# Sums of v on GpSimd for all pairs, joined bits from the second pair on, and another instruction order for hashed attention with a channel mix behind it

## The chip, the cores and the metric

The kernel runs on one core of one Trainium2 chip. Times are device microseconds (us) of one execution. TensorE is called PE, VectorE DVE, ScalarE ACT and GpSimd POOL, as in the profile. A time "timed" is of an ordinary execution, a "profiled" one of the execution that the trace shows; "span" is the stretch from its first to its last instruction. Every execution also has a mean granted clock of TensorE (1.0 is full speed) and a state, fast or slow (here: over 1.5% above the fastest of the same kernel).

## The reference, cut to what matters

```python
# attention: 4 batches x 8 heads, 768 positions, 64 wide
q_bits = (q @ proj > 0); k_bits = (k @ proj > 0)          # 6 bits each
mask   = bucket(q_bits)[:, None] == bucket(k_bits)[None]   # attend only within a bucket
attn   = softmax(where(mask, q @ k.T / 8, -1e9))
x      = (attn @ v)  laid out as [batch, 768, 512]
# channel mix ("feed-forward" below)
x_prev = x shifted by one position
xk = mu_k * x + (1 - mu_k) * x_prev ;  xr = mu_r * x + (1 - mu_r) * x_prev
k  = relu(xk @ w_k) ;  v = (k * k) @ w_v ;  r = sigmoid(xr @ w_r)
out = r * v                                                # float32
```

## The kernel before

Work comes in 16 pairs of heads, four pairs to a batch; pair 3 ends batch 0, and only when the mix of pair 3 is there can the first feed-forward matmul run. Each pair needs: loads of q, k and v; two DVE operations that split q and k into a float16 high and low part; a DMA transpose (for pairs 0 and 1 a transpose on PE); the hash bits, found by small matmuls and written as extra rows of the operands; nine score blocks and nine exponentials; the weighted sums of v; a division; a transposition; a difference and a mix.

All instructions are first collected as operations with an engine, a priority and an estimated duration. A plan then simulates the engines and emits the instructions in the order that it found. The priorities are a long list of numbers found by search.

```python
WANT = [4, 17, 6, 12, ...]            # 1306 priorities, cut
...
    def schedule(self):
        ...
                if o.tr:               # a DMA transpose
                    dur = max(dur, dma_free - 1.0 - t, tr_free + 0.1 - t)
```

The sums of v over the 768 positions give the mean, which is subtracted from v (pairs 4 to 15) or added as a tiny term (pairs 0 to 3, "uc"):

```python
        def f1(): nc.gpsimd.tensor_tensor(... 128x390 ...)     # three adds, pairs 0 to 3
        def f2(): nc.gpsimd.tensor_tensor(... 128x130 ...)
        def f3(): nc.gpsimd.tensor_tensor(... 128x130 ...)
        def f123():                                            # one reduction, pairs 4 to 15
            nc.vector.tensor_reduce(out=vs, in_=vn.rearrange("p j c d -> p j d c"), axis=X, op=ALU.add)
        ...                       # then: mean on PE, subtraction ("va") and "mc" on DVE
```

Bits are written in one of two ways. `DIRECT` pairs get them on the spot, one DVE operation of 6 rows for each of the four operands. All others get "joined" bits: one DVE operation for all four, `bx`, followed by four small row DMAs that put the rows in place.

```python
    DIRECT = (0, 1)
```

The weights w_r and w_v are staged in float32 in the buffer that later holds the squares of the feed-forward, and cast from there:

```python
    k2_f = k2_all.bitcast(FP32)                      # k2: squares of relu
    ...
        if z < NST: stage = k2_f[:, z * 2 * DM : (z + 1) * 2 * DM]     # w_r 0,2 and w_v 0,2
        else:       stage = wst[...]                                     # w_v 4,6
        add("SP", 0.5, T, f_w, ...)       # the load, named wl4 to wl9
        add("POOL", 1.1, ..., f_c, ...)   # the cast, named wc4 to wc9
```

The softmax here doesn't subtract the row's maximum and nothing guards it: scores larger than these inputs give would overflow.

Of the kernel before, what the change touches and what calls it, by code (L numbers as in the profile page):

```python
# [39 lines left out]
def R(kind, n):  # L40
# [4 lines left out]
    4, 17, 6, 12, 16, 19, 26, 30, 33, 21, 5, 14, 18, 20, 8, 10, 24, 13, 7, 9, 22, 25, 29, 27,  # L45
    23, 70, 31, 32, 34, 37, 38, 28, 74, 2, 41, 122, 57, 65, 127, 252, 271, 299, 321, 353, 378, 287, 307, 390,
    413, 435, 430, 0, 11, 1, 15, 58, 35, 3, 66, 36, 39, 44, 48, 55, 63, 42, 45, 49, 60, 40, 43, 47,
    54, 62, 68, 46, 50, 59, 53, 56, 61, 71, 84, 94, 80, 67, 69, 83, 89, 99, 79, 96, 86, 136, 85, 92,
    98, 102, 77, 72, 78, 100, 123, 141, 51, 52, 64, 88, 106, 111, 76, 93, 101, 73, 126, 133, 87, 117, 129, 139,
    143, 156, 103, 107, 81, 91, 90, 97, 75, 82, 121, 124, 138, 140, 132, 134, 113, 119, 110, 114, 149, 135, 146, 130,  # L50
    151, 145, 152, 155, 170, 177, 182, 197, 209, 212, 224, 221, 109, 128, 105, 104, 108, 112, 115, 95, 125, 142, 118, 144,
    153, 174, 180, 203, 189, 198, 194, 148, 158, 159, 164, 147, 150, 169, 178, 165, 171, 195, 200, 188, 191, 179, 183, 161,
    168, 184, 190, 192, 211, 215, 204, 207, 210, 232, 239, 241, 246, 249, 250, 262, 257, 116, 202, 120, 154, 157, 163, 167,
    131, 137, 162, 160, 166, 175, 199, 205, 245, 225, 234, 217, 226, 231, 235, 237, 248, 253, 229, 259, 238, 242, 213, 219,
    220, 218, 216, 227, 206, 208, 270, 273, 277, 292, 293, 251, 254, 258, 276, 279, 322, 329, 334, 337, 351, 342, 176, 186,
    222, 173, 181, 187, 214, 172, 185, 233, 230, 236, 244, 263, 272, 289, 278, 290, 283, 268, 286, 280, 285, 275, 267, 260,
    269, 256, 264, 288, 312, 282, 291, 298, 301, 243, 247, 294, 302, 309, 314, 324, 313, 317, 326, 332, 347, 352, 359, 363,
    366, 371, 422, 381, 387, 404, 410, 419, 445, 436, 441, 456, 392, 398, 406, 420, 439, 446, 492, 499, 506, 449, 468, 481,
    407, 415, 429, 448, 466, 480, 451, 516, 526, 479, 486, 500, 438, 457, 473, 509, 515, 532, 514, 528, 536, 489, 504, 519,
    476, 483, 494, 524, 531, 533, 548, 571, 578, 505, 510, 574, 587, 605, 612, 577, 581, 561, 563, 588, 623, 636, 650, 632,  # L60
    642, 652, 704, 627, 631, 590, 597, 645, 694, 647, 656, 660, 670, 686, 793, 223, 261, 274, 296, 303, 305, 311, 323, 193,
    196, 201, 228, 240, 265, 295, 300, 330, 297, 343, 320, 316, 325, 344, 348, 335, 333, 339, 341, 328, 349, 304, 308, 310,
    318, 355, 357, 350, 354, 356, 360, 365, 376, 383, 368, 373, 380, 386, 388, 327, 416, 444, 453, 469, 503, 461, 475, 346,
    370, 377, 340, 345, 379, 391, 402, 255, 266, 338, 281, 284, 306, 385, 393, 412, 408, 424, 400, 389, 394, 362, 367, 375,
    382, 403, 409, 395, 401, 372, 374, 414, 426, 397, 421, 417, 433, 423, 425, 427, 434, 458, 465, 467, 474, 478, 484, 442,
    488, 517, 523, 544, 543, 535, 551, 384, 361, 428, 315, 331, 358, 336, 364, 399, 437, 455, 405, 411, 443, 497, 508, 518,
    530, 513, 525, 459, 472, 440, 452, 470, 477, 454, 460, 485, 495, 502, 507, 511, 521, 431, 447, 482, 490, 522, 529, 520,
    539, 547, 537, 540, 546, 553, 558, 369, 562, 583, 595, 601, 609, 611, 658, 319, 396, 463, 418, 491, 557, 564, 568, 450,
    487, 501, 432, 527, 534, 567, 576, 580, 594, 584, 602, 538, 542, 545, 549, 555, 559, 573, 586, 582, 591, 596, 604, 570,
    575, 593, 598, 552, 556, 603, 606, 608, 615, 621, 613, 616, 619, 624, 626, 655, 629, 653, 662, 675, 679, 692, 697, 710,  # L70
    682, 729, 701, 711, 731, 716, 728, 770, 707, 695, 717, 734, 747, 761, 746, 762, 796, 696, 786, 795, 771, 779, 822, 756,
    783, 799, 817, 823, 831, 791, 797, 818, 805, 828, 839, 829, 838, 847, 850, 859, 869, 812, 830, 837, 836, 842, 855, 803,
    810, 870, 874, 883, 887, 785, 794, 888, 895, 903, 913, 833, 890, 867, 886, 917, 925, 926, 933, 919, 912, 936, 945, 967,
    976, 975, 983, 986, 991, 943, 953, 923, 931, 962, 968, 471, 464, 572, 462, 554, 566, 599, 651, 498, 560, 565, 493, 579,
    589, 622, 633, 644, 659, 639, 663, 665, 671, 610, 614, 620, 625, 646, 661, 640, 649, 657, 666, 638, 643, 630, 634, 674,
    684, 678, 680, 683, 688, 693, 723, 725, 727, 733, 735, 767, 742, 773, 777, 784, 790, 787, 792, 496, 541, 617, 512, 654,
    677, 669, 685, 550, 628, 635, 569, 637, 648, 691, 700, 718, 709, 721, 713, 708, 714, 706, 722, 699, 702, 668, 676, 687,
    690, 720, 732, 749, 757, 738, 741, 730, 737, 740, 743, 750, 758, 763, 766, 769, 801, 814, 820, 775, 835, 864, 872, 881,
    889, 876, 897, 600, 607, 698, 592, 705, 712, 724, 754, 585, 641, 673, 618, 703, 726, 778, 800, 815, 808, 811, 821, 760,
    764, 755, 772, 804, 819, 802, 813, 782, 789, 781, 806, 745, 752, 845, 851, 827, 834, 843, 852, 858, 875, 878, 880, 893,  # L80
    899, 907, 910, 774, 915, 929, 932, 940, 944, 935, 977, 689, 667, 788, 664, 826, 856, 848, 862, 672, 719, 751, 715, 739,
    759, 816, 832, 853, 844, 860, 849, 861, 868, 892, 896, 906, 911, 854, 863, 894, 901, 840, 846, 879, 884, 904, 908, 877,
    882, 957, 960, 963, 971, 974, 934, 948, 952, 959, 966, 873, 978, 990, 992, 995, 1001, 999, 1006, 1126, 1130, 1133, 1020, 1025,
    1030, 1078, 1087, 1094, 1042, 1049, 1059, 1132, 1141, 1146, 1026, 1035, 1044, 1095, 1103, 1109, 1047, 1063, 1066, 1122, 1150, 1152, 1110, 1116,
    1121, 1015, 1114, 1119, 1074, 1080, 1084, 1145, 1155, 1157, 1104, 1124, 1128, 1134, 1139, 1143, 1092, 1100, 1111, 1031, 1039, 1162, 1169, 1173,
    1175, 1089, 1091, 1149, 1179, 1176, 1180, 1174, 1182, 1154, 1159, 1185, 1187, 1202, 1207, 1197, 1200, 1209, 1210, 1194, 1198, 1183, 1206, 1215,
    1216, 1212, 1213, 1226, 1229, 1232, 1235, 681, 768, 866, 744, 898, 909, 914, 924, 748, 753, 776, 765, 809, 825, 918, 902, 942,
    954, 937, 949, 981, 985, 916, 920, 964, 970, 980, 982, 955, 961, 972, 979, 930, 941, 950, 969, 939, 946, 994, 998, 1000,
    1004, 1009, 988, 1003, 1005, 1011, 1013, 927, 1017, 1033, 1036, 1055, 1061, 1046, 1054, 736, 798, 922, 841, 938, 947, 956, 965, 780,
    824, 871, 807, 900, 905, 1010, 1016, 1040, 1029, 1023, 1034, 993, 996, 997, 1007, 984, 989, 1045, 1051, 1014, 1018, 1008, 1012, 1038,  # L90
    1043, 1022, 1027, 987, 1002, 1057, 1062, 1069, 1073, 1075, 1050, 1056, 1067, 1072, 1077, 973, 1081, 1097, 1098, 1102, 1115, 1105, 1113, 921,
    1019, 1024, 1021, 1028, 857, 865, 958, 885, 891, 928, 1086, 1090, 1107, 1101, 1112, 1096, 1068, 1076, 1060, 1064, 1106, 1118, 1082, 1085,
    1079, 1083, 1065, 1071, 1053, 1070, 1088, 1093, 1099, 1108, 1137, 1140, 1142, 1147, 1151, 1123, 1117, 1120, 1125, 1127, 1032, 1153, 1165, 1161,
    1166, 1170, 1167, 1214, 951, 1037, 1048, 1041, 1052, 1138, 1144, 1164, 1168, 1148, 1156, 1129, 1131, 1135, 1136, 1181, 1184, 1158, 1160, 1163,
    1171, 1172, 1178, 1177, 1186, 1188, 1190, 1192, 1189, 1191, 1193, 1195, 1196, 1058, 1199, 1201, 1203, 1204, 1205, 1208, 1219, 1224, 1211, 1218,
    1221, 1217, 1222, 1225, 1223, 1227, 1230, 1239, 1244, 1246, 1234, 1238, 1240, 1220, 1228, 1231, 1237, 1241, 1243, 1251, 1256, 1258, 1248, 1253,
    1255, 1245, 1250, 1252, 1242, 1247, 1249, 1257, 1262, 1264, 1260, 1265, 1267, 1254, 1259, 1261, 1266, 1271, 1273, 1263, 1268, 1270, 1274, 1277,
    1272, 1276, 1278, 1280, 1233, 1236, 1269, 1275, 1281, 1284, 1286, 1282, 1287, 1295, 1294, 1296, 1279, 1285, 1283, 1288, 1290, 1291, 1300, 1298,
    1297, 1301, 1304, 1305, 1289, 1292, 1293, 1299, 1302, 1303,
]  # L100


class Op:
    pass


class Plan:
# [15 lines left out]
    def add(self, eng, dur, prio, fn, r=(), w=(), take=None, give=(), lag=None, name="", at=0.0, svc=0.0, off=None, tr=0, port=0):  # L123
        o = Op()
# [789 lines left out]
```

## Time and profile before

| what | before |
|---|---|
| timed, two runs | 261.88 and 261.82 us |
| profiled run: time, span, granted clock | 258.05, 256.3, 0.989 |
| first feed-forward matmul | 69.1 us |
| PE busy ahead of it | 56.4 of 69.1 us |
| PE busy after it, up to PE's end | 180.0 of 182.6 us |
| PE's end to the end of the span | 4.6 us |

The table's last rows come from the busy times by stretch. The columns are: the stretch and its length, then busy us (and instructions) of PE, PE's weight loads, DVE, ACT and POOL, then the granted clock, the DMA share and GB/s. The kernel before:

```profile
0.00:69.10 69.10, 56.44 (x678) 35.33 (x679) 58.75 (x106) 50.08 (x57) 20.72 (x50) 0.98 0.99 242
69.10:251.67 182.57, 180.03 (x1761) 106.50 (x1776) 140.50 (x326) 133.78 (x186) 4.72 (x3) 1.00 0.59 143
251.67:256.30 4.63, 0.00 (x0) 0.00 (x0) 0.69 (x1) 0.00 (x0) 0.00 (x0) 0.77 0.29 113
```

PE stands idle for 12.7 us in the first stretch and for 2.5 us in the second.

One more view of the kernel before, the same columns at 2 us: PE has a bubble at 32 to 36 us, and its clock is granted at half at 36 to 38 us.

```profile
32.00:34.00 2.00, 1.30 (x23) 0.68 (x20) 0.10 (x1) 1.83 (x2) 0.00 (x0) 1.00 1.25 216
34.00:36.00 2.00, 0.78 (x14) 0.43 (x13) 1.79 (x3) 0.04 (x1) 0.00 (x0) 0.92 1.00 294
36.00:38.00 2.00, 2.00 (x20) 1.25 (x17) 1.68 (x5) 0.00 (x0) 0.42 (x1) 0.50 0.83 237
```

### The profile page before, as it was taken

The page shows a single profiled execution, that of the slowest core. Times are in us where ns is not written, and L with a number is a line of the kernel's source. Part 1 is how long each engine was busy: PE and PEld are TensorE (multiplying, and loading weights), DVE is VectorE, ACT ScalarE, POOL GpSimd, SP SyncE. Part 2 cuts the span into 40 slices and gives each one's busy share as a digit, 9 for nine tenths or more (in the row PEclk, how much of TensorE's full clock was granted, in tenths as well). Part 3 has the DMA queues.
Part 4 walks back from the last instruction along what each step waited for, and adds up shares of the span by engine and source line. Part 5 has one row for each costly group of instructions (what it writes and reads, how often), then busy time and mean ns, then how long its engine had stood idle before and what let it go on. Part 6 is the DMA issues. An engine that isn't in the chain of part 4 may idle for free.

```text
span 256.3 us, 6102 instructions
## 1 busy us (share of the span) xinstructions
PE 236.5 (92%) x2434; PEld 141.8 (55%) x2453; DVE 199.9 (78%) x431; ACT 183.9 (72%) x241; POOL 25.4 (10%) x53
## 2 busy tenths in 40 slices
PE   7688978897999999999999989999999999999992
PEld 3445544564665565556575455466575656555440
DVE  3999968799999999998987997995976644755322
ACT  4673939899889966669797976579899866257210
POOL 6181800111023000000000000000000000000000
PEclk9999979999999999999999999999999999999998
DMA  6999999989999978896999966868101013030122
GB/s 180 259 380 230 197 239 208 252 246 209 296 289 228 248 185 175 225 229 139 280 253 178 272 89 166 166 185 171 36 6 33 7 31 120 6 122 3 71 92 82
DMA packets 73291, 43.44 MB, mean 170 GB/s; under 512 B 55520, under 2 KB 68144, under 8 KB 73264
## 3 DMA queue, kind: packets, MB, share of 16 engines
q1 hardware_dynamic: 72608, 42.02, 66.9%
q0 software_dynamic: 576, 1.05, 2.2%
q8 instruction: 19, 0.31, 0.5%
q14 instruction: 8, 0.07, 0.1%
q10 hardware_dynamic: 80, 0.00, 0.0%
HBM read 24.12 MB, written 6.29 MB: 119 GB/s over the span
## 4 chain that ended last, share of the span: by engine, by line
PE 69%; DMA 12%; DVE 9%; SPq 4%; ACT 3%; issue 2%; DVEq 0%; ACTq 0%
PE ps_all L698 16%; PE ps_all L847 16%; PE ps_all L818 13%; PE ps_all L728 11%; PE ps_all L837 7%; DMA a<-bx 5%; PE ps_all L582 4%; DMA a<-nh 3%; ACT pt L702 3%; DMA xt<-ob 2%; DMA nat<-in_k_dram 2%; SPq L595 1%; DVE a L666 1%; DVE vs L517 1%; DVE nh L621 1%
## 5 line engine op out<-in xcount | busy, mean ns | idle before, releaser
L702 ACT ACTIVATE pt<-ps_all 128x1024 bf16<-128x1024 f32 x144 | 141.4, 1031 | 32.5 <-PE ps_all L698 31.5
L698 PE MATMUL ps_all<-a 128*128 128x512 f16 (+1 forms) x384 | 82.3, 327 | 5.2 <-ACT pt L702 2.7
L728 PEld LDWEIGHTS <-pt 128*128 128x128 bf16 x1152 | 44.7, 98 | 8.7 <-issue 0.5
L698 PEld LDWEIGHTS <-a 128*128 128x128 f16 x384 | 32.9, 97 | 28.8 <-issue 9.1
L818 PE MATMUL ps_all<-xk,wk 128*128 128x384 bf16 x256 | 48.0, 326 | 0.4 <-ACT kr L822 0.4
L728 PE MATMUL ps_all<-va,pt 128*128 128x65 bf16 x1152 | 46.7, 194 | 0.1
L847 PE MATMUL ps_all<-wv,k 128*128 128x512 bf16 x181 | 45.8, 379 | 0.6
L822 ACT ACTIVATE kr<-ps_all 128x384 bf16<-128x384 f32 x64 | 30.4, 498 | 7.6 <-PE ps_all L818 5.9
L818 PEld LDWEIGHTS <-wk 128*128 128x128 bf16 x256 | 24.4, 98 | 16.9 <-issue 1.0
L854 DVE SCALAR_TENSOR_TENSOR os<-rs,ps_all 128x512 f32<-128x512 f32 x24 | 16.3, 684 | 19.0 <-PE ps_all L847 12.6
L840 ACT ACTIVATE rs<-ps_all 128x512 f32<-128x512 f32 x24 | 14.4, 599 | 22.8 <-PE ps_all L837 22.7
L847 PEld LDWEIGHTS <-k 128*128 128x128 bf16 x192 | 18.5, 98 | 19.7 <-issue 0.3
L825 DVE TENSOR_TENSOR k<-kr 128x384 bf16<-128x384 bf16 x64 | 21.8, 351 | 9.5 <-ACT kr L822 9.4
L559 DVE SCALAR_TENSOR_TENSOR nh<-nat,nh 128x768 f16<-128x768 f32 x28 | 27.4, 980 | 0.1
L837 PE MATMUL ps_all<-wr,xr 128*128 128x512 bf16 x88 | 24.1, 379 | 0.4
L556 DVE TENSOR_SCALAR nh<-nat 128x768 f16<-128x768 f32 x28 | 15.7, 563 | 4.0 <-DMA nat<-in_q_dram 1.9
L517 DVE TENSOR_REDUCE vs<-vn 128x128 bf16<-128x768 f32 x12 | 17.8, 1479 | 0.3 <-DMA vn<-in_v_dram 0.3
L744 DVE TENSOR_TENSOR ob<-ps_all,rc 128x384 bf16<-128x384 f32 x32 | 17.6, 553 | 0.4
L585 DVE TENSOR_SCALAR bx<-ps_all 128x768 uint16<-128x768 uint16 x14 | 13.3, 953 | 3.3 <-PE ps_all L582 3.1
L837 PEld LDWEIGHTS <-xr 128*128 128x128 bf16 x96 | 9.2, 98 | 10.0 <-issue 0.3
L582 PE MATMUL ps_all<-a,p 128*32 128x256 f16 (+1 forms) x224 | 12.4, 331 | 2.2 <-DMA a<-nh 1.9
L538 DVE SCALAR_TENSOR_TENSOR va<-ps_all,vn 128x384 bf16<-128x384 f32 x24 | 12.8, 545 | 0.2 <-PE ps_all L533 0.2
(67 smaller groups left out, 151.2 us busy)
## 6 DMA issues: line engine op xcount, KB each, us to landing
vn<-in_v_dram SPq DMA_DIRECT2D x16, 384.0 KB
out_dram<-os SPq DMA_DIRECT2D x24, 256.0 KB
nat<-in_k_dram SPq DMA_DIRECT2D x15, 384.0 KB
nat<-in_q_dram SPq DMA_DIRECT2D x15, 384.0 KB
wk<-in_moe_w_k_dram POOLq DMA_DIRECT2D x4, 256.0 KB, 7.8
k<-in_moe_w_r_dram SPq DMA_DIRECT2D x2, 512.0 KB
k<-in_moe_w_v_dram SPq DMA_DIRECT2D x2, 512.0 KB
wst<-in_moe_w_v_dram SPq DMA_DIRECT2D x2, 512.0 KB
```

The source lines that it names most:

```text
L517: nc.vector.tensor_reduce(out=vs, in_=vn.rearrange("p j c d -> p j d c"), axis=mybir.AxisListType.X, op=ALU.add)
L559: nc.vector.scalar_tensor_tensor(out=nh[:, :, D:P], in0=nat.rearrange("p j (c d) -> p (j c) d", d=D), scalar=QS, in1=nh[:, :, 0:D], op0=AL ...
L582: nc.tensor.matmul(ps[32 * i : 32 * i + 32, lo:hi], w_, a_t[sa][:, i, lo:hi], start=st, stop=not st)
L698: nc.tensor.matmul(ps[:, lo - s * STEP : hi - s * STEP], side_a["k"][sa][:, j, jc * P : (jc + 1) * P], side_a["q"][sa][:, j, q0 : q0 + hi ...
L702: nc.scalar.activation(out=pt_t[sp][:, s * STEP : (s + 1) * STEP], in_=ps_t[plan.slot[nm]], func=AF.Exp, bias=EBIAS, scale=ESC)
L728: nc.tensor.matmul(oo[:, ic * 65 : ic * 65 + 65], pt_t[sp][:, o : o + P], va_t[sa][:, j, jc, 0 : D + 1], start=(not uc and ic == 0 and jc ...
L744: nc.vector.tensor_tensor(out=ob_t[so][:, :, j * D : (j + 1) * D], in0=oo[:, :, 0:D], in1=rc_t[sr][:, 1, :].unsqueeze(2).to_broadcast([P, ...
L818: nc.tensor.matmul(ps[:, 0:HALF], wk_sb[:, d, fc * P : (fc + 1) * P], xk_t[mx[d]][:, h * HALF : (h + 1) * HALF], start=(d == 0), stop=(d = ...
L822: nc.scalar.activation(out=kr_t[sk], in_=sm(nm)[:, 0:HALF], func=AF.Relu, scale=0.5 ** 0.5)
L825: nc.vector.tensor_tensor(out=k2_t[s2][:, h * HALF : (h + 1) * HALF], in0=kr_t[sk], in1=kr_t[sk], op=ALU.mult)
L837: nc.tensor.matmul(sm(nr), xr_t[mx[d]][:, c * P : (c + 1) * P], wr_sb[:, d, :], start=(d == 0), stop=(d == NDC - 1))
L847: nc.tensor.matmul(sm(nv), k2_t[(b * NFC + fc) % NK2][:, c * P : (c + 1) * P], wv_sb[:, fc, :], start=(fc == 0), stop=(fc == NFC - 1))
```

## The change

Its intent: take the twelve reductions off DVE, which is the fullest engine early on, and give them to GpSimd, which is idle nine tenths of the time; take the bits of pair 1 from four DVE operations to one; and tell the plan that a DMA transpose behind a backlog of transfers takes longer, then search the order anew.

```diff
-WANT = [4, 17, 6, 12, ...]          # 1306 priorities
+WANT = [6, 17, 10, 0, ...]          # 1328 priorities, all others
...
                 if o.tr:
+                    dma_free += 0.5 * (dma_free > t)
...
+                heapq.heappush(events, (t + dur, 3, o.i))
...
-    DIRECT = (0, 1)
+    DIRECT = (0,)
...
-        add("SP", ..., svc=1.08, name=f"ldq{n}{side}")
+        add("SP", ..., svc=1.13, name=f"ldq{n}{side}")     # and small changes of other estimated costs
...
-        def f123(): ... nc.vector.tensor_reduce(...)
-        if not uc:
-            add("DVE", DVE_C(768), pr, f123, ...)
-        else:
-            add("POOL", 0.85, pr, f1, ...)   # and f2, f3
+        add("POOL", 0.85, pr, f1, ...)       # and f2, f3, for all pairs
```

## The prediction

> **What bounds the kernel now.** I read the busy table first, then stretches of time, then the DVE groups, then the chain of waits and the timelines of the first 70 us.
>
> ```profile
> PE 236.5 (92%) x2434; PEld 141.8 (55%) x2453; DVE 199.9 (78%) x431; ACT 183.9 (72%) x241; POOL 25.4 (10%) x53
> ...
> PE   7688978897999999999999989999999999999992
> ...
> DVE  3999968799999999998987997995976644755322
> ```
>
> TensorE is busy 92% of 256.3 us, and the digits show that nearly all of what is missing lies in the first ten or eleven slices (6.4 us each), before the first feed-forward work. There DVE stands at 9. The stretches make this exact; 69.20 us is where the first feed-forward matmul starts (from the timeline of PE), 251.70 us where PE ends. Columns: stretch, its length, then PE, PEld, DVE, ACT, POOL busy us with counts, granted clock, DMA share, GB/s.
>
> ```profile
> 24.00:32.00 8.00, 7.42 (x106) 4.98 (x106) 7.33 (x11) 6.69 (x8) 5.94 (x7) 1.00 1.05 171
> 32.00:40.00 8.00, 6.08 (x82) 4.06 (x79) 5.57 (x10) 2.96 (x4) 0.42 (x1) 0.79 1.03 228
> 40.00:48.00 8.00, 5.80 (x54) 3.28 (x52) 5.49 (x12) 8.00 (x9) 0.00 (x0) 1.00 1.03 200
> 48.00:56.00 8.00, 7.90 (x129) 5.10 (x127) 7.90 (x13) 7.18 (x9) 1.61 (x1) 1.00 0.97 285
> 56.00:64.00 8.00, 6.43 (x86) 4.24 (x82) 8.00 (x15) 7.47 (x8) 2.08 (x2) 1.00 1.00 211
> ...
> 69.20:251.70 182.50, 179.93 (x1758) 106.45 (x1774) 140.40 (x325) 133.68 (x185) 4.72 (x3) 1.00 0.59 143
> ```
>
> From 69.2 us on PE is full (179.93 of 182.50), whatever the others do: that part can only move as a block. Before it PE is busy 56.5 of 69.2 us, 12.7 us idle. So the kernel's end is "when does feed-forward work start" plus a fixed amount of PE work. Two things set that start. First, at 32 to 40 us ACT has 2.96 us of work: a gap of 4.29 us before its 19th exponential, which waits for the scores of pair 2, and PE waited for the transpose DMA:
>
> ```profile
> 30.01 5.17 DMA a<-nh
> 35.22 1.06 PE ps_all L582 x8
> ```
>
> Second, by the timeline of ACT the 36th exponential (the last of pair 3) ends near 56.8 us, yet the first feed-forward matmul starts 12.4 us later, because its input, the mix of pair 3, is the last of a long DVE queue; 56 to 64 us has DVE at 8.00 of 8.00, with the sums of v in it:
>
> ```profile
> 57.78 1.38 DVE vs L517
> ...
> 60.88 0.54 DVE va L538
> 61.42 0.47 DVE df L785
> 61.88 1.37 DVE vs L517
> 63.26 0.93 DVE xr L791
> ```
>
> **What the Trainium skill says.** "VectorE: DVE Perf Modes", the perf-mode tier table: a tensor_reduce has only the 1x rate. The trace is even worse than one element a cycle: 768 float32 take 1479 ns, while the two-input operation on as many elements takes 980.
>
> ```profile
> L559 DVE SCALAR_TENSOR_TENSOR nh<-nat,nh 128x768 f16<-128x768 f32 x28 | 27.4, 980 | 0.1
> L517 DVE TENSOR_REDUCE vs<-vn 128x128 bf16<-128x768 f32 x12 | 17.8, 1479 | 0.3 <-DMA vn<-in_v_dram 0.3
> L666 DVE TENSOR_SCALAR a<-ps_all 6x768 uint16<-6x768 uint16 x6 | 5.6, 953 | 0.3
> L507 POOL TENSOR_TENSOR vt<-va 128x390 f32<-128x390 bf16 x4 | 3.6, 898 | 0.3
> L510 POOL TENSOR_TENSOR vt<-vt 128x130 f32<-128x130 f32 x4 | 2.0, 499 | 0.3
> ```
>
> "GPSIMD Engine Reference", 3.1, puts a GpSimd add at about twice the Vector engine's time; here 390 columns take 0.85 us undisturbed, and the engine is 90% idle, so twice is cheap. "SBUF — State Buffer", Who interferes with whom: GpSimd shares a port pair with DVE operations that have two SBUF inputs or run in a two-port mode, as an exclusive lock, and tensor_reduce never takes part. The trace agrees: the last add of a pair takes 0.42 us alone and 1.01 us at 27.6 us beside DVE work, and the DVE subtraction of 384 columns takes 1.05 us at 12.3 us beside GpSimd against 0.55 usually. "TensorE: Matmul & The Clock Gate", Part 1: the clock follows recent activity. The trace shows 0.79 in 32 to 40 us, the stretch with the transpose wait, so a bubble there costs more than itself.
>
> **The change part by part.** (1) Twelve reductions leave DVE: 12 x 1479 ns = 17.8 us. Twelve groups of three adds come to GpSimd: 0.85 + 0.42 + 0.42 = 1.7 us, 20 us in all on an engine with 25.4 us of work. Some of it comes back to DVE as lock time; the four groups of the kernel before lengthened DVE operations by some 0.3 us a group (my estimate from the durations above), so 12 x 0.3 = 3.6 us, mostly after 69 us where it does not matter. (2) Pair 1 no longer writes its bits in place: four DVE operations of 0.95 us and 32 small matmuls go; one joined operation (0.9 us), 16 joined matmuls (0.8 us) and four small row DMAs come, which must queue behind other transfers. (3) The plan's cost for a transpose behind a backlog rises, so the whole order is another one. This is the largest part, and it can be read from the built instruction order: the first feed-forward matmul comes after 42 score blocks instead of 48 and before the weighted sums of pair 4; on DVE, everything of v's means (pairs 4 to 6) now stands behind the mix of pair 3.
>
> DVE work that must precede the mix of pair 3: before, from 3.13 to 68.39 us less 6.4 us of waits in the DVE timeline, 58.9 us. Taken away: 4 x 0.95 = 3.8 for the bits, 3 x 1.4 = 4.2 for the sums of pairs 4 to 6 (1.37 to 1.43 start to start), 2.2 for subtracting the means of pairs 4 and 6, moved behind; added 0.9. 58.9 - 9.3 = 49.6 us, so DVE alone would allow 52.7 us.
>
> But the exponentials must also come. I walked the new order by hand with the durations of the trace. The first exponential starts about 0.5 us later (10.9), as DVE does more of pair 1 first. The second head of pair 0 gets its bits near 19 us (29 DVE operations, 14.7 us of work from 3.1 us and 1.5 us of waits) instead of 16.4 to 17.3; so ACT pauses after four exponentials, and the ninth ends near 24.7 us (23.2 before). The rows of pair 1, issued from 17.3 us, should be there by then, and the eighteenth ends near 33.3 us (34.0 before). The bits of pair 2 come near 29.8 us, their rows near 35, so the nineteenth starts near 36 us instead of 38.3, the twentieth near 37 instead of 39.9. At 0.945 us each (11 in 10.40 us) the 36th ends near 53 us. Then the last weighted sum (1.5 us), division, joined bits and second division (2.6), the transposing matmuls behind three score blocks, the copy, the difference and the mix (2.7): the first feed-forward matmul near 60.1 us, 9.1 us earlier than now.
>
> Of that, PE work that now stands behind instead of ahead is paid back: 6 score blocks x 0.43 + the weighted sums of pair 4, 2 x 1.15, + two means, 0.2: 5.1 us. Gain 9.1 - 5.1 = 4.0 us. The tail (PE's end to the span's end, 4.6 us) keeps its length. 261.85 - 4.0 = 257.8 us.
>
> **The rivals.** (a) A DMA wait takes the place of the DVE wait. For it: the DMA share is near 1.0 from 8 to 140 us, total bytes do not fall, four row DMAs are added, and all four weight loads on the GpSimd queue now stand at the start. Then the rows of pairs 1 and 2 come 2 to 4 us later than I took and the gain is 0 to 2 us: 260 to 262. Against it: fewer loads stand ahead of the first transposes in the new order. (b) The plan is now right about transposes and the gap before the nineteenth exponential vanishes altogether: the 36th ends near 51 us, feed-forward starts at 57 to 58, the gain is 6 to 7 us: 255 to 256. For it: the DVE floor of 52.7 us allows it. Against: the bits still take a DVE queue, a small DMA and about 5 us. (c) Later starvation: PE is ahead by several us but pairs 8 to 13 still come at the DMA's pace, and PE idles at 120 to 160 us, where the chain already shows transposes of 3.68 and 4.43 us. That would return 1 to 3 us. (d) GpSimd's in-order queue: sums behind a weight cast that waits for its DMA (the old kernel waited up to 12.7 us there) delay a mean. Unlikely to bind, as v has three buffers and means stand far ahead.
>
> **Range and chances.** 257.8 us, with 254.6 to 260.6 holding it 8 times in 10: (b) sets the low end, (a) and (c) the high one. Faster by 2% means under 256.6, a gain over 5.2 us; with an uncertainty of some 2.7 us around 4.0 that is about one chance in three. Slower by 2% would need a new stall of 9 us in a freshly laid order: 3%.
>
> **What would show it.** Right: the reduction gone, DVE near 180 us busy, POOL near 46; the first feed-forward matmul near 60 us, the gap before the nineteenth exponential under 3 us, the clock at 32 to 40 us above 0.79, PE full after. Wrong if that matmul starts after 63 us, if PE after it is idle by over 4 us more than the 2.6 us now, or if adds on GpSimd average far over 0.6 us and stretch DVE's subtractions above 1.1 us.

## The result, and the profile after

The changed kernel took 258.10 and 257.71 us, 257.9 in the middle, and agrees with the reference. Against the kernel before in the same rounds its ratio is 0.9849, with a 95% interval of 0.9807 to 0.9892. Here and below a ratio is the mean time of one kernel's fast runs over that of the other's fast runs of the same rounds, so it is not quite the ratio of the medians that are quoted. By the mark of 2% that the prediction used, this counts as the same time: the gain is clear of noise, but it is not shown to reach 2%.

The page of the changed kernel: busy times, then PE, DVE and granted clock in 40 slices, in tenths.

```profile
PE 234.8 (92%) x2433; PEld 140.3 (55%) x2453; DVE 186.6 (73%) x416; ACT 182.9 (71%) x241; POOL 48.3 (19%) x89
...
PE   8769987797997999899899999999999999999993
...
DVE  3997889889667986998999848668764656673422
...
PEclk9999999999999999999999999999999999999999
```

DVE lost 13.3 us of work and POOL gained 22.9. A slice is 6.4 us. PE's line now has holes behind the tenth slice: a 7 in the 13th (77 to 83 us), an 8 in the 17th and the 20th, where the kernel before had nines up to the 23rd. The clock line has no dip; that of the kernel before had a 7 in its sixth slice (and an 8 in its last). By stretches, the changed kernel:

```profile
0.00:59.70 59.70, 48.84 (x587) 29.62 (x588) 48.97 (x88) 42.18 (x49) 20.35 (x52) 1.00 0.98 225
59.70:252.42 192.72, 185.92 (x1850) 110.64 (x1867) 136.96 (x328) 140.73 (x193) 27.90 (x38) 1.00 0.65 153
252.42:256.20 3.78, 0.00 (x1) 0.00 (x0) 0.69 (x1) 0.00 (x0) 0.00 (x0) 0.92 0.36 139
```

The four terms: the start came 9.4 us earlier (69.1 to 59.7), PE work after it grew by 5.9 (180.03 to 185.92), idle time of PE after it grew by 4.3 (2.54 to 6.80), the tail shrank by 0.85. The sum is -0.1 us: **the two profiled runs are equally long** (256.3 and 256.2), while the timed runs differ by 4 us. So this pair of profiles cannot explain the gain. One of them, that of the kernel before, is of a run that was far better than its usual.

Why it starts earlier is seen in ACT's timeline (start, length, line, operation, how many; in brackets the idle time before, and what ended it). In the kernel before, the 19th exponential and the eight from the 31st to the 38th:

```profile
38.33 1.02 ACT L702 ACTIVATE pt<-ps_all 128x1024 bf16<-128x1024 f32 x1 [4.29 <-PE ps_all L698]
...
51.01 7.66 ACT L702 ACTIVATE pt<-ps_all 128x1024 bf16<-128x1024 f32 x8 [0.67 <-PE ps_all L698]
```

The changed kernel:

```profile
10.56 3.77 ACT L700 ACTIVATE pt<-ps_all 128x1024 bf16<-128x1024 f32 x4
19.41 13.01 ACT L700 ACTIVATE pt<-ps_all 128x1024 bf16<-128x1024 f32 x14 [5.07 <-PE ps_all L696]
34.27 1.02 ACT L700 ACTIVATE pt<-ps_all 128x1024 bf16<-128x1024 f32 x1 [1.86 <-PE ps_all L696]
36.01 12.02 ACT L700 ACTIVATE pt<-ps_all 128x1024 bf16<-128x1024 f32 x13 [0.71 <-PE ps_all L696]
...
50.36 2.85 ACT L700 ACTIVATE pt<-ps_all 128x1024 bf16<-128x1024 f32 x3 [0.66 <-PE ps_all L696]
```

Four exponentials, a pause, then fourteen in a row: the 18th ends at 32.4 us, the 19th starts at 34.3 after 1.86 us of idleness (4.29 before), and the 36th ends at 53.2 instead of 56.8. The first feed-forward matmul then follows 6.5 us after the 36th exponential; before it was 12.3. Both stretches, the gap before the 19th exponential and the one after the 36th, are thus shorter. Which part of the change shortened them is a matter for the experiments.

Where the new idle time lies: the stretches of 20 us from 80 to 140 us, the kernel before first.

```profile
80.00:100.00 20.00, 19.84 (x219) 12.40 (x224) 19.67 (x47) 16.45 (x24) 1.04 (x1) 1.00 0.98 211
100.00:120.00 20.00, 19.89 (x188) 11.06 (x191) 18.14 (x35) 14.50 (x17) 0.00 (x0) 1.00 0.92 205
120.00:140.00 20.00, 19.86 (x260) 13.10 (x260) 17.27 (x43) 17.89 (x25) 0.00 (x0) 1.00 1.00 228
```

The changed kernel:

```profile
80.00:100.00 20.00, 17.51 (x186) 9.90 (x187) 16.65 (x40) 11.58 (x18) 3.86 (x6) 1.00 1.10 238
100.00:120.00 20.00, 18.87 (x164) 10.57 (x164) 18.79 (x38) 17.70 (x21) 5.74 (x8) 1.00 0.99 239
120.00:140.00 20.00, 18.85 (x243) 11.71 (x243) 18.67 (x45) 15.19 (x21) 0.00 (x0) 1.00 0.92 199
```

PE falls from 59.59 to 55.23 of 60 us. (At 140 to 160 us it is the kernel before that idles: PE is busy 18.74 of 20 us there, and 19.78 in the changed kernel.) The largest single wait in there has its cause in the staged weights. The chain of waits of the changed kernel (start, length, what):

```profile
70.45 7.00 DMA k<-in_moe_w_r_dram
77.51 1.05 POOL wr L464
```

and the timelines of DVE, ACT and PE in the same kernel, one line of each:

```profile
78.58 0.36 DVE L823 TENSOR_TENSOR k<-kr 128x384 bf16<-128x384 bf16 x1 [3.75 <-POOL wr L464]
...
82.64 0.49 ACT L820 ACTIVATE kr<-ps_all 128x384 bf16<-128x384 f32 x1 [2.04 <-DVE k L823]
...
83.18 2.03 PE L835 MATMUL ps_all<-wr,xr 128*128 128x512 bf16 x7 [1.75 <-ACT kr L820]
```

The new order issues a load of w_r at 70.45 us. It lands 7.0 us later, GpSimd casts it, and only then may DVE write squares to the buffer in which it was staged; DVE stands for 3.75 us, a relu on ACT waits 2.04 us for DVE to free its buffer, and PE waits 1.75 us for the relu. Each link passes on less than it got.

What the adds cost on GpSimd (the groups of its own instructions; after the bar busy us and mean ns, then idle time before and its releaser):

```profile
L511 POOL TENSOR_TENSOR vt<-vn 128x384 f32<-128x384 f32 x12 | 13.3, 1106 | 68.0 <-DMA vn<-in_v_dram 67.8
L514 POOL TENSOR_TENSOR vt<-vt 128x128 f32<-128x128 f32 x12 | 6.3, 529 | 0.9
L517 POOL TENSOR_TENSOR vs<-vt 128x128 bf16<-128x128 f32 x12 | 5.2, 436 | 10.5 <-PE ps_all L531 9.6
```

That is 2.07 us a group and 24.8 us for twelve. For most of its idle time GpSimd waits for v to land. Only one wait of PE for a sum, of 1.03 us at 62.84 us, is of any size.

### The profile page after: what moved, and what is told of

It is laid out like the page before. It is cut to its first block, busy times and chain, and to the rows that moved or that the text cites. A ratio compares the mean times of both kernels' runs of the same rounds, so it can differ in the third digit from the quotient of the medians.

```text
span 256.2 us, 6145 instructions
## 1 busy us (share of the span) xinstructions
PE 234.8 (92%) x2433; PEld 140.3 (55%) x2453; DVE 186.6 (73%) x416; ACT 182.9 (71%) x241; POOL 48.3 (19%) x89
## 4 chain that ended last, share of the span: by engine, by line
PE 45%; DVE 20%; DMA 19%; SPq 7%; issue 3%; POOL 2%; ACT 2%; DVEq 0%; POOLq 0%
PE ps_all L845 12%; PE ps_all L696 10%; PE ps_all L816 9%; PE ps_all L726 7%; PE ps_all L835 5%; DMA a<-nh 5%; SPq L593 4%; DMA nat<-in_k_dram 4%; DVE nh L557 4%; DMA vn<-in_v_dram 3%; DMA k<-in_moe_w_r_dram 3%; DVE bx L583 2%; DVE nh L554 2%; ACT pt L700 2%; DMA xt<-ob 2%
## 5 line engine op out<-in xcount | busy, mean ns | idle before, releaser
L696 PE MATMUL ps_all<-a 128*128 128x256 f16 (+1 forms) x384 | 80.8, 325 | 7.0 <-DMA a<-bx 2.6
L696 PEld LDWEIGHTS <-a 128*128 128x128 f16 x384 | 33.7, 97 | 34.2 <-issue 9.4
L726 PEld LDWEIGHTS <-pt 128*128 128x128 bf16 x1152 | 43.5, 97 | 11.1 <-issue 4.2
L726 PE MATMUL ps_all<-va,pt 128*128 128x65 bf16 x1152 | 45.3, 193 | 1.0 <-DVE ob L742 1.0
L820 ACT ACTIVATE kr<-ps_all 128x384 bf16<-128x384 f32 x64 | 31.4, 513 | 10.7 <-PE ps_all L816 7.3
L823 DVE TENSOR_TENSOR k<-kr 128x384 bf16<-128x384 bf16 x64 | 22.7, 363 | 18.8 <-ACT kr L820 15.0
L511 POOL TENSOR_TENSOR vt<-vn 128x384 f32<-128x384 f32 x12 | 13.3, 1106 | 68.0 <-DMA vn<-in_v_dram 67.8
L852 DVE SCALAR_TENSOR_TENSOR os<-rs,ps_all 128x512 f32<-128x512 f32 x24 | 16.4, 683 | 13.2 <-PE ps_all L845 10.9
L583 DVE TENSOR_SCALAR bx<-ps_all 128x768 uint16<-128x768 uint16 x15 | 14.3, 950 | 2.1 <-PE ps_all L580 1.1
L580 PE MATMUL ps_all<-a,p 128*32 128x256 f16 (+1 forms) x240 | 13.1, 328 | 0.4 <-DMA a<-nh 0.4
```

Source lines behind the costliest of these rows:

```text
L583: nc.vector.tensor_scalar(out=bx_t[sx].bitcast(U16), in0=ps_t[plan.slot[nm]][:, 0:S].bitcast(U16).rearrange("p (c e) -> p c e", e=2)[:, :, 1],
L696: nc.tensor.matmul(ps[:, lo - s * STEP : hi - s * STEP], side_a["k"][sa][:, j, jc * P : (jc + 1) * P], side_a["q"][sa][:, j, q0 : q0 + hi ...
L726: nc.tensor.matmul(oo[:, ic * 65 : ic * 65 + 65], pt_t[sp][:, o : o + P], va_t[sa][:, j, jc, 0 : D + 1], start=(not uc and ic == 0 and jc ...
L820: nc.scalar.activation(out=kr_t[sk], in_=sm(nm)[:, 0:HALF], func=AF.Relu, scale=0.5 ** 0.5)
L823: nc.vector.tensor_tensor(out=k2_t[s2][:, h * HALF : (h + 1) * HALF], in0=kr_t[sk], in1=kr_t[sk], op=ALU.mult)
```

## The experiments

The question: of an order that starts the feed-forward earlier, sums moved to GpSimd, and joined bits of pair 1, which one carries the 4 us? The account of the prediction: DVE work that stood ahead of the mix of pair 3 is gone, so the feed-forward starts earlier, and what DVE does later does not matter. First rival: the order alone brings the start forward, and the sums matter later, or not at all. Second rival: the gain is the clock, that is, the bubble at 32 to 36 us and its throttled stretch. Twelve kernels ran, in three groups, each group on another chip with its own runs of the kernel before.

All twelve were timed in five rounds, six executions each with the profiled one; medians and ranges are of all six, slow ones too. "Start" is the first feed-forward matmul and "idle" PE's idle time from there to its end, both of the profiled run.

| run | order | sums (pairs 4 to 15) | bits of pair 1 | median (range), us | ratio to before, 95% | start | idle |
|---|---|---|---|---|---|---|---|
| r1_before_again | old | DVE | direct | 261.51 (259.64 to 263.89) | 1.0004, 0.9933 to 1.0075 | slow run | |
| r1_before_pool_sums | old | GpSimd | direct | 262.54 (260.11 to 263.00) | 1.0038, 0.9971 to 1.0104 | 70.0 | 4.1 |
| r2_old_order_joined1 | old | DVE | joined | 264.81 (263.32 to 266.60) | 1.0149, 1.0102 to 1.0197 | 74.4 | 4.6 |
| r3_old_no_sums | old | none | direct | 259.84 (257.68 to 261.56) | 0.9961, 0.9911 to 1.0012 | 70.3 | 4.2 |
| r2_new_order_neither | new | DVE | direct | 262.29 (258.93 to 264.44) | 1.0065, 1.0014 to 1.0117 | 60.7 | 5.2 |
| r1_after_dve_sums | new | DVE | joined | 261.84 (261.06 to 263.21) | 1.0045, 0.9982 to 1.0108 | 60.8 | 8.2 |
| r2_new_order_direct1 | new | GpSimd | direct | 258.88 (256.96 to 259.70) | 0.9901, 0.9854 to 0.9948 | 62.0 | 4.7 |
| r1_after_again | new | GpSimd | joined | 257.07 (255.74 to 258.45) | 0.9844, 0.9784 to 0.9904 | 59.5 | 5.6 |
| r3_new_early_sums_dve | new | DVE for 4 to 7 | joined | 259.95 (258.46 to 261.36) | 0.9995, 0.9950 to 1.0039 | 60.7 | 7.4 |
| r3_new_late_sums_dve | new | DVE for 8 to 15 | joined | 259.94 (257.80 to 260.73) | 0.9985, 0.9936 to 1.0034 | 59.9 | 6.7 |
| r3_new_no_sums | new | none | joined | 257.55 (254.84 to 257.99) | 0.9880, 0.9833 to 0.9927 | 59.4 | 5.9 |
| r2_new_order_weights_swapped | new | GpSimd | joined | 258.31 (255.28 to 259.85) | 0.9852, 0.9796 to 0.9909 | 58.2 | 4.35 |

One ratio needs care. That of `r2_new_order_neither`, 1.0065, counts two runs (264.44 and 263.69), slow beside its best, 258.93, and leaves that best one out. From the four runs marked fast, 261.23 us on average against 261.11, it is 1.000. "No faster than before" holds either way; "slower" does not.

### Both kernels again

No edit.

> The kernel before, unchanged, timed five times with the span of every run. Its profiled run took 258.05 us (span 256.3) but its two timed runs 261.82 and 261.88, while the changed kernel was profiled at 258.1 and timed at 257.71 to 258.1. Theory A (the old order has two outcomes, DMA arrivals decide which): the runs scatter between about 258 and 262, and more than one in five lies over 260. Theory B (it is a matter of the one profile): all runs lie within 0.5 us of 261.85 and a new profile shows a span near 260, with feed-forward work starting later than 69.2 us or PE idle after it.

> The changed kernel, unchanged. Theory A: its runs lie within 0.7 us of 257.9, ratio to before 0.985 to 0.99 if before mostly lands high. The new profile shows again the first feed-forward matmul near 59.7 us and about 5 us of idle PE at 80 to 140 us.

The gain stands: 0.9844. But the kernel before scatters: its eleven runs of this group go from 259.26 to 266.20 us, where the changed kernel's six keep within 2.7 us (the six of `r1_before_again` within 4.3). So Theory B is out, and the scatter of Theory A is there and wider than expected; that DMA arrivals cause it is not shown. For the changed kernel the expectation missed in part: four of its six runs lie below the 257.2 to 258.6 us that were expected, and PE idles 3.4 us at 80 to 140 us instead of about 5. The new profile of the kernel before fell in a slow run (263.89, clock 0.987), so it is not used against fast ones. The new profile of the changed kernel gives start 59.5, PE 186.13 of 191.76 (idle 5.6), tail 3.84, span 255.1. The wait for the staged weights is there again but smaller, 2.3 us on DVE and 0.31 us on PE: its size changes from run to run.

With runs by the dozen the clock can be held against the time. Of 39 runs of the kernel before (three groups and the six here), 31 were fast; those with a mean granted clock under 0.9885 (a split that was not fixed beforehand) took 261.67 us on average (13 runs), the others 260.21 (18 runs). The changed kernel's six runs have a mean clock of 0.997, the seven fast runs of before in the same group 0.989. So the clock goes along with some 1.5 us of the 4; a straight line through the 31 runs gives 0.9 us for the same difference of clock. It is not all: at a like clock (0.989 to 0.993) the four runs of before in this group average 260.25 us and the two of the changed kernel 257.86, which leaves 2.4 us. This is a correlation; no run set the clock. One run further down speaks against the clock as the main cause: with the new order and the sums on DVE, the six runs had a mean clock of 0.996 and still took 262.1 us on average, where the changed kernel took 256.9 at 0.997 on the same chip.

### The old order with the sums on GpSimd

```diff
         def f123():
-            nc.vector.tensor_reduce(...)
+            f1(); f2(); f3()          # the GpSimd adds, at the same places of the old order
```

> The old order, with the twelve reductions alone put on GpSimd as three adds at the same places. Theory 1 (DVE in 54 to 69 us bounds the start of feed-forward work): three reductions of 1.4 us leave DVE there, feed-forward starts up to 3 us earlier, ratio 0.985 to 0.992. Rival (the GpSimd queue holds the sums behind weight casts that wait for their DMA, so means come later): the ratio is 0.998 to 1.02, and the profile shows means waiting for GpSimd.

Nothing was gained: 1.0038. DVE has 56.56 us of work ahead of the feed-forward instead of 58.75, yet that starts at 70.0 us. PE now waits for GpSimd where it had the sums before. PE's timeline of this run, then GpSimd's:

```profile
65.20 0.22 PE L533 MATMUL ps_all<-vs,ones 128*128 128x128 bf16 x1 [1.41 <-POOL vs L513]
```

```profile
61.27 1.04 POOL L460 CAST wr<-k 128x1024 bf16<-128x1024 f32 x1
62.27 1.31 POOL L507 TENSOR_TENSOR vt<-vn 128x384 f32<-128x384 f32 x1
63.65 1.01 POOL L510 TENSOR_TENSOR vt<-vt 128x128 f32<-128x128 f32 x1
64.74 0.41 POOL L513 TENSOR_TENSOR vs<-vt 128x128 bf16<-128x128 f32 x1
```

The sums stand behind a weight cast in GpSimd's queue, and the adds are stretched beside DVE work (1.31 and 1.01 us, against 1.00 and 0.41 for the group before them): the mean comes late, and PE waits for it with score blocks behind it. That is rival (d) of the prediction, seen in the old order. It is not shown to be what holds the start, though: with no sums at all, further down, the old order starts at 70.3 us as well. In the new order the means stand behind the mix of pair 3 and cannot delay its start.

### The new order with the sums back on DVE

```diff
         def f1(e=nc.gpsimd):
+            if not uc:
+                nc.vector.tensor_reduce(out=vs, ...)    # and f2, f3 do nothing
+                return
```

> The new order, with the twelve sums put back on DVE as reductions at the same places. Theory 1: in the new order the sums of pairs 4 to 7 stand after the mix of pair 3, where DVE has slack (75% busy), so little of the 17.8 us comes back: 257.9 to 260. Rival (DVE bounds the stretch 80 to 140 us, where it was 92% busy): 261 us or more.

The whole gain is gone (1.0045), though the feed-forward starts at 60.8 us, still 8 to 9 us earlier than in the old order. The stretches from the start to PE's end show where it went, the changed kernel again first, this run second:

```profile
59.50:251.26 191.76, 186.13 (x1850) 110.79 (x1867) 137.73 (x328) 140.84 (x193) 28.54 (x38) 1.00 0.64 155
```

```profile
60.80:255.55 194.75, 186.54 (x1849) 110.75 (x1867) 148.33 (x341) 140.18 (x192) 5.22 (x5) 1.00 0.63 152
```

DVE has 10.6 us more to do after the start, and PE's idle time goes from 5.6 to 8.2 us. The span is 4.8 us longer: 1.3 from the start, 2.6 from this idle time, 0.4 from PE work, 0.5 from the tail. So DVE work after the start does matter, in an order that starts early. The order was searched for sums on GpSimd, however, and not searched again for this run; the same holds, the other way round, for the run before. Over the six runs the clock was about as high as in the changed kernel (0.996 and 0.997), so it can hardly be the cause of these 2%.

Of the prediction's two reasons for the late start, this run bears on the second, that the sums stand in DVE's queue ahead of the mix of pair 3. With the sums back on DVE the 36th exponential ends at 54.1 us and the feed-forward follows 6.7 us later, as in the changed kernel (6.5) and not as in the kernel before (12.3). So it is the order that shortens this stretch.

### The new order with the bits of pair 1 in place, and with neither

```diff
-    DIRECT = (0,)
+    DIRECT = (0, 1)      # the eight operations of direct bits, in place of six, get priorities right behind the bits of pair 0
```

For "neither", the edit of the run before it on top.

> The new order and the GpSimd sums, but pair 1 writes its bits in place again (four DVE operations of 0.95 us, standing where the joined one and its neighbours stood, and no row DMAs for pair 1). Theory D (the joined bits are worth their DVE time, 3.8 - 0.9 = 2.9 us before the mix of pair 3): feed-forward starts 1 to 3 us later than 59.6 us and the ratio to before is 0.99 to 0.995. Rival (DVE is not what sets the first 30 us; the row DMAs cost as much as they save): the ratio stays at 0.982 to 0.988.

> The new order with both parts undone: sums on DVE, bits of pair 1 in place. If the order alone were the gain, 257 to 259. From the run with the sums put back (261.84) and theory D I expect 262 to 265, no better than before: the order pays only with the work taken off DVE.

Direct bits with the sums on GpSimd give 0.9901; the start moves from 59.5 to 62.0 us, as Theory D had it. In time the joined bits may be worth about 0.6% (0.9844 against it), but that is not clear of noise: the two were timed on two chips and their intervals overlap. Where the sums are on DVE no difference is shown (1.0045 against 1.0065). With neither, the order by itself starts the feed-forward at 60.7 us and is no faster at all than the kernel before: 1.0065. The profile of that run is of its best execution (258.93; the median is 262.29), so its idle time of 5.2 us is not typical of it, and no more is read from it.

This is the run that separates start from time: **over 8 us of earlier start came to nothing in time.** The run with the sums on DVE shows where such a lead goes, in an execution near its median. Beside the old order with sums on GpSimd it starts 9.2 us earlier, has 6.4 us more PE work left then, 4.1 us more idle time and 0.3 us more tail. Work that moves behind the start has to be done there, and only what is left of the lead can be a gain.

### The old order with joined bits for pair 1

```diff
-    DIRECT = (0, 1)
+    DIRECT = (0,)        # the joined operation right behind the last transposed copy of pair 1
```

> The old priorities and the sums on DVE, with joined bits for pair 1 alone. Theory D: up to 2.9 us less DVE work, ratio 0.99. Rival (in the old order the rows of pair 1 stand behind the many loads issued early, up to the loads of pair 4, so pair 1 comes late): the first exponential of pair 1 starts after 28 us instead of 25, ratio 1.0 to 1.015.

Slower by 1.5%. ACT's timeline of this run:

```profile
17.48 4.69 ACT L702 ACTIVATE pt<-ps_all 128x1024 bf16<-128x1024 f32 x5 [0.34 <-PE ps_all L698]
29.91 6.63 ACT L702 ACTIVATE pt<-ps_all 128x1024 bf16<-128x1024 f32 x7 [7.74 <-PE ps_all L698]
```

Before the first exponential of pair 1, ACT waits 7.74 us: the rows now come by small DMAs, and the old order has no other exponentials for that time. PE too waits 3.55 us up to 28.10 us. The start moves to 74.4 us. Three operations saved on DVE cost 4 us when their result is at once on the path.

### The new order with loads of the weights exchanged

```diff
     order = plan.schedule()
+    at = {o.name: i for i, o in enumerate(order)}
+    for x, y in (("wl5", "wl9"), ("wc5", "wc9"), ("wl6", "wl8"), ("wc6", "wc8")):
+        order[at[x]], order[at[y]] = order[at[y]], order[at[x]]
```

The late load is now of weights that are not staged in the buffer of squares.

> The changed kernel with the second half of the r weights loaded and cast where a part of the v weights was, and the other way round, twice (its load issued near 52 us instead of 70). Theory W (the idle PE at 80 to 100 us, 1.5 to 2.5 us, comes from DVE waiting 2.3 to 3.8 us for the cast of the r weights out of the buffer that the squares are to be written to): that wait is gone, PE idles under 1 us at 80 to 100 us, 0.5 to 2 us faster than the changed kernel: ratio to before 0.976 to 0.982. Rival (that wait only takes the place of another, the loads of q and k that DVE waits for next): ratio 0.983 to 0.987.

The 3.75 us wait of DVE for the cast is gone from the list of waits, and so is the 1.75 us of PE. The time is the same: 0.9852 against 0.9844. PE is busy 18.43 of 20 us at 80 to 100 us (18.50 in the second profile of the changed kernel), and its longest wait there is now this one:

```profile
97.36 0.61 PE L696 MATMUL ps_all<-a 128*128 128x512 f16 x2 [1.34 <-DMA a<-bx]
```

It waits for the row DMAs of a later pair, and waited 0.58 us for them before the exchange. A wait that was removed gave way to the next one. Our reading is that PE has by then caught up with what DVE and the transfers can bring; it agrees with the small size of the removed wait in the changed kernel's second profile (0.31 us). One execution of this kernel took 255.28 us, near the shortest seen, but its median is not better than that of the changed kernel.

### Which of the sums count

```diff
+            if 4 <= n < 8:        # early; the late run has: if n >= 8
+                nc.vector.tensor_reduce(out=vs, ...)
+                return
```

> The changed kernel with the sums of pairs 4 to 7 alone back on DVE, those of pairs 8 to 15 on GpSimd. The prediction's step (only the sums before the mix of pair 3 matter; those after 69 us do not) would have nearly all of the loss here; but in the new order even these stand after that mix, so it predicts no loss: ratio 0.984 to 0.988. Theory E (all DVE work up to about 125 us counts, as the transposes of pairs 7 to 12 wait for DVE): four of the eight reductions of that stretch stand here, so half of the 2% is lost: 0.992 to 0.998.

> The changed kernel with the sums of pairs 8 to 15 alone back on DVE. The prediction's step: no loss, 0.984 to 0.988. Theory E: the other half, 0.992 to 0.998, with 1.5 to 3 us more idle PE at 100 to 125 us than the changed kernel and the start of feed-forward work unchanged at 59 to 60 us.

And no sums at all, in either order: a constant is written in place of the sum. The mean is then wrong, though the comparison with the reference still passed.

```diff
+            if not uc:
+                nc.gpsimd.memset(vs, 0.0)
+                return
```

> The changed kernel with each group of three adds replaced by a memset of the sums to zero on GpSimd (a wrong result on purpose). Theory E: the adds themselves cost little where they are (some 3.6 us of stretched DVE operations in all, one wait of about 1 us of PE for a sum at 62 us): 0 to 1.5 us faster than the changed kernel, ratio 0.979 to 0.985. Rival (the lock between the two engines still costs a lot): 0.975 or less.

> The kernel before with the reductions replaced by the same memset (a wrong result on purpose): DVE loses 17.8 us and GpSimd gains nothing. Theory F (in the old order the sums on GpSimd brought nothing because they stood behind weight casts and held the mix of pair 3): this run is 1 to 2% faster than before, 0.98 to 0.99. Rival (the old order is held by its transposes and rows, not by DVE work): 0.995 to 1.005, and feed-forward still starts near 70 us.

In the new order four early reductions cost 1.2% over no sums (0.9995 over 0.9880), eight late ones 1.1% (0.9985 over 0.9880); each interval is half a per cent wide to either side, so they are alike and both there. That is what Theory E expected of each half, if a little more: both ratios to before lie just above its range of 0.992 to 0.998. Its other marks were met by the late sums: the start stays at 59.9 us, and PE is busy 17.35 us at 100 to 120 us, against 18.97 with no sums.

With none, 0.9880 is close to what the changed kernel showed on the other chip (0.9844, overlapping): twelve groups on GpSimd cost no time that can be seen here (the expectation of 0.979 to 0.985 was too low). The changed kernel was not run in this group, so no finer comparison is made.

In the old order, taking all 17.8 us of reductions away brings 0.4%, which is within the noise (up to 0.9% by the interval), and the feed-forward starts at 70.3 us. So Theory F failed and its rival held. There DVE's sums are not what sets the start. ACT's timeline of that run shows both gaps of the kernel before still in place:

```profile
40.61 1.02 ACT L701 ACTIVATE pt<-ps_all 128x1024 bf16<-128x1024 f32 x1 [5.06 <-PE ps_all L697]
...
53.05 7.62 ACT L701 ACTIVATE pt<-ps_all 128x1024 bf16<-128x1024 f32 x8 [0.61 <-PE ps_all L697]
```

The 19th exponential waits 5.06 us, the 36th ends at 58.7 us, and the feed-forward follows 11.6 us later. The two runs without sums, on one chip, also show best what the order is worth once DVE is relieved: the new one starts 10.9 us earlier, has 6.7 us more PE work left, 1.7 us more idle time and 0.2 us less tail, so its span is 2.8 us shorter.

The waits of PE with the early sums on DVE:

```profile
62.60 0.32 PE L824 MATMUL ps_all<-xk,wk 128*128 128x384 bf16 x1 [1.22 <-DVE xk L797]
65.93 0.81 PE L824 MATMUL ps_all<-xk,wk 128*128 128x384 bf16 x4 [1.25 <-DVE mc L551]
```

and with the late sums on DVE:

```profile
114.32 1.02 PE L853 MATMUL ps_all<-wv,k 128*128 128x512 bf16 x4 [1.16 <-DVE mc L551]
```

`mc` is the end of the work on a pair's mean, and `xk` the mix: DVE's queue with the reduction in it. In the changed kernel PE waits 0.20 us at 114.33 us, and 1.03 us at 62.84, there for the sum on GpSimd.

## Why the prediction was right or wrong

**The time, 257.8 against 257.9, and the start, 60.1 against 59.7 and 59.5: right.** The walk through the new order held at each stage: first exponential 10.9 (10.56), 18th ends 33.3 (32.4), 19th starts 36 (34.3), 36th ends 53 (53.2). The gap before the 19th is under 3 us, and the clock is full at 32 to 40 us, both as it said. DVE's work ahead of the start, expected at 49.6 us, is 48.97.

**PE work paid back, 5.1 us: 5.9** (180.03 to 185.92), near enough.

**DVE's time given back: the term was right, the level was not.** It expected DVE near 180 us; it is 186.6. By the lengths of the single operations, 17.8 us of reductions and 3.8 of bits go and 1.0 for one joined operation comes, 20.6 us less, of which 13.3 are seen. But not all of the missing 7.3 us came back by the lock. The page of the new order with no sums at all reads:

```profile
PE 234.4 (92%) x2433; PEld 140.5 (55%) x2453; DVE 183.2 (72%) x416; ACT 182.6 (71%) x241; POOL 26.9 (11%) x65
```

So the twelve groups of adds cost DVE 3.4 us (183.25 to 186.62), or 3.9 in the second profile (187.15), where the prediction had put 3.6. The operations with two inputs are longer beside them: the difference 604 ns instead of 554, the last step of the mix 628 instead of 552. The rest is missing without any adds too. Part of it is the counting: the records of neighbouring operations overlap (a reduction of 1.46 us at 57.70 us has the next operation start 1.37 us after it), so that the lengths add up to more than the busy time. The adds themselves take 24.8 us of GpSimd where 20 had been put.

**"That part can only move as a block" and "PE full after": wrong.** This is the step that failed. The prediction made the end of the kernel the start of the feed-forward plus a fixed amount of PE work, "whatever the others do". PE's idle time after the start was taken as unchanged. It grew from 2.5 to 6.8 us in the first profile, over the mark that the prediction itself had set (4 us over 2.6), and to 5.6 in the second; against the other fast profiles of the old order, which have 4.1 to 4.6, it is 1.0 to 2.7 us more. Rival (c), starvation later on, came true, only at 80 to 140 us instead of 120 to 160. Starting earlier puts PE ahead of pairs that come at the pace of DVE and of the transfers, and part of the lead is lost there. DVE's sums are one cause: with them on DVE the idle time is 8.2 us. But with no sums at all 5.9 us remain, and what causes these is not separated. The chain that ended last shows the same: PE is 64 to 71% of it in the fast profiles of the old order, but 45 and 59% in the two of the changed kernel.

**What DVE's relief is good for: wrong too,** and from the same cause. The prediction wrote "mostly after 69 us where it does not matter" of the lock time, and of that it holds: twelve groups of adds cost no time that can be seen. But it took all DVE work after the start to be free, and counted the relief only ahead of the feed-forward, 4.2 us of sums. In the old order it was worth nothing that can be seen, even with every sum gone (start 70.3, ratio 0.9961). In the new order it is worth 2.0% in time (sums on DVE give 1.0045, on GpSimd 0.9844) but only 1.3 us of the start (60.8 to 59.5): early and late sums count alike. The order by itself, which the prediction called the largest part, makes nearly all of the earlier start and gives no gain in time (1.0065, with the care that is noted below the table).

So the sum came out right with errors that offset each other, and the agreement to 0.1 us is in part luck. The lead of the feed-forward was taken as kept, though some of it is lost to waits later. And the 4.0 us were read in a profile of 258.05 us but subtracted from the usual 261.85 us; against the profile itself the changed kernel gained nothing. The usual run of the kernel before is worse than the one on which the sum was built. Beside the fast profile of the old order with sums on GpSimd (same time as before in its ratio: start 70.05, PE 180.15 of 184.24, tail 4.06, span 258.3) the changed kernel's second profile has: start 10.6 us earlier, PE work 6.0 more, idle 1.5 more, tail 0.2 less, together 3.2 us. This pairing is of two kernels and serves as a size only.

**What stays open.** Why the kernel before scatters by over 7 us (39 executions) and the changed one by under 3 (six). The clock goes along with part of it: every profile of the old order has a throttled stretch within its first 45 us and the two of the changed kernel have none, but some of the other kernels in the new order have one too (that with the sums on DVE at about 39 to 45 us). That the removed bubble is the cause is argued, not shown. Also open: how much of the order is due to the plan's new cost of a transpose and how much to the new priorities, as the two were not run apart. And neither order was searched again for the crossed runs, so they show what each part is worth in these two orders, not what the best order for it would give.

## What to carry to other kernels

When the fullest engine is fed by others, an earlier start is worth only as much as its feeders keep up with afterwards: run the new order without the relief and the relief without the new order, since here each alone gave no gain that was clear of noise and both together 1.6%. An operation moved to an idle engine must also be placed: the same adds that cost no visible time in one order stood behind a cast in the other, and TensorE waited 1.41 us for one of them. And before building a sum on a profile, check that the profiled run took what the timed runs take.

## What the Trainium skill lacked or had wrong

- "TensorE: Matmul & The Clock Gate", Part 1: it says that the throttle works on a free-running window of about 3.4 us and comes back after an idle one. Here PE's least busy 3.4 us around the bubble of the kernel before (32.3 to 35.7 us) have it busy for 1.49 us, and the clock was 0.50 at 36 to 38 us; in the changed kernel PE was busy 1.00 us of 3.4 at 15.4 to 18.8 us, and the clock stayed at 1.00. A free-running window may allow both, but the page gives no busy share below which a window counts as idle, and these two show that PE need not stand idle for a whole window.
- "VectorE: DVE Perf Modes", perf-mode tier table: it puts tensor_reduce and tensor_tensor on float32 at the same 1x. Here the reduction of 768 float32, read at a stride of 64 elements, took 1479 ns, and a scalar_tensor_tensor on 768 (one input float32, one float16) took 980. The table says nothing of strided reads, so the tier alone misleads here; other pages of the skill do treat them, and no run here shows whether the stride is the cause.
- No page: how far executions of one unchanged kernel on one core scatter. Here 39 of them went from 258.62 to 266.20 us, and the first profile (258.05) was of one shorter than all of these.
